# Head of an attention-plus-gated-MLP kernel: one load on another queue, one sum split around a transpose, three weight tiles for one

## The chip, the cores and the metric

The kernel runs on one core of one Trainium2 chip. A core has a matrix engine (TensorE, PE in the profile, with weight loads shown apart as PEld), a vector engine (VectorE, DVE), a scalar engine (ScalarE, ACT), GpSimdE (POOL) and a sync engine (SP). Each has its own instruction stream and runs it in order; they meet through semaphores. Transfers between memory and on-chip buffers are issued as instructions by SP, and a few by ACT; their issue shows in the profile as SPq and ACTq. The metric is the device time of one execution in microseconds (us). A nanosecond is written ns.

## The reference

One sequence of 2048 rows with 640 features is normalised row by row and goes through two branches, whose sums are added to the input:

```python
xn = _layernorm(x)                       # mean 0, variance 1 per row
qkv = xn @ wqkv                          # 640 x 1920: 32 heads of 20 for q, k and v
scores = q @ k.T * 20 ** -0.5            # a query sees the last 256 keys up to itself
o = softmax(masked scores) @ v           # per head
h = _sigmoid(xn @ w_gate) * (xn @ w_up)  # 640 x 1536 each
out = x + o @ wo + h @ w_down
```

Inputs, weights and output are bf16.

## The kernel before, in words

The 2048 rows are cut into four chunks of 512, and a chunk into four blocks of 128 rows. A chunk is normalised, transposed into `xnT` (features on partitions), projected to Q, K and V, and used for the gated MLP; attention runs in steps over head groups, and the MLP, the later projections and the output products are dealt out between these steps by a small planner (`Fill`) when the program is built. The schedule is written by hand: every engine gets its instructions in the order of the Python program, and nothing reorders them on the chip.

Only the head of the program is touched by the change, the first 13 us or so, in which chunk 0 is loaded, normalised and projected to V:

* **Loads.** SP issues, in this order: blocks 0, 1 and 3 of x (line 157, 160 KB each), the first half of the V columns of `wqkv` (line 161, 400 KB), block 2 of x, the second V half, then the Q and the K columns (line 151, 800 KB each). After these come MLP weights and the clearing of scratch rows. Since SP's instruction stream is in order, a later line is issued after the earlier ones.
* **Warm-up.** TensorE multiplies constants (line 233, ten 512-column products) until the first rows are there. ScalarE's first instruction is a load of its function table for the square root, placed ahead of a dummy activation (line 229) that reads `eps`, which POOL fills.
* **Normalising chunk 0.** Blocks 0 and 3 get mean and variance on VectorE (`ln_half`, `ln_mv`, lines 253 and 259); blocks 1 and 2 get theirs on ScalarE by two passes with accumulation (`mean_act`, line 620, and `root_act`, lines 625 and 626). `root` (line 610) is a square root on ScalarE, `norm` and `norm_act` (lines 614, 273, 630, 631) finish on VectorE.
* **Transposes.** `transpose_rows` (lines 280 and 281) turns a normalised block by five TensorE products with the identity, into a PSUM tile, and copies it to `xnT`; block 0 in pieces of three and two columns-of-128 by ScalarE, the other blocks whole by VectorE. These are called t0 to t3 below.
* **V.** `project_v` (line 329) makes one half (320 columns) of V for one block by five products; Vsh below is block s, half h (V00, V01, ..., V31). `copy_v` (line 338) brings the sums from PSUM into the V tiles, split between VectorE and ScalarE.

The order of TensorE's work in the head is: warm-up, t0, t1, V00, V10, t3, V01, V30, V11, t2, V31, V20, V21. After that come the Q and K projections of chunk 0 (`proj_block`, line 300), which read Q and K columns of the same weight tile, and then the long mixed part. The one weight tile `wqkv` has 3 x 640 columns for each of the five 128-feature slices.

Of the kernel before, what the change touches and what calls it, by code (L numbers as in the profile page):

```python
# [9 lines left out]
P = 128  # L10
S = 2048
D = 640
# [3 lines left out]
DC = D // P  # L16
FC = F // P
CW = 512
# [7 lines left out]
HALF = 320  # L26
# [11 lines left out]
BF16 = mybir.dt.bfloat16  # L38
FP32 = mybir.dt.float32
EXP = mybir.ActivationFunctionType.Exp  # L40
TANH = mybir.ActivationFunctionType.Tanh
SQRT = mybir.ActivationFunctionType.Sqrt
# [51 lines left out]
def kernel(  # L94
# [11 lines left out]
    nc = tc.nc  # L106
# [4 lines left out]
    def pool(name, bufs, **kw):  # L111
        return ctx.enter_context(tc.tile_pool(name=name, bufs=bufs, **kw))

    const = pool("const", 1)
# [13 lines left out]
    ps_d = pool("ps_d", 4, space=bass.MemoryType.PSUM)  # L128
# [10 lines left out]
        xc[c] = t  # L139
        nc.sync.dma_start(out=t, in_=xr[:, c * SBC:(c + 1) * SBC, :])  # L140

    wqkv = const.tile([P, DC, 3 * D], BF16, name="wqkv")
    wqkv_r = A_wqkv.rearrange("(c p) n -> p c n", p=P)
    wg = [const.tile([P, DC, FS], BF16, name=f"wg{k}") for k in range(F // FS)]
    wu = [const.tile([P, DC, FS], BF16, name=f"wu{k}") for k in range(F // FS)]
# [2 lines left out]

    ones = nc.const_aps.tensor(1.0, [P, CW], BF16)
    def load_wqkv(part):  # L150
        nc.sync.dma_start(out=wqkv[:, :, part * D:(part + 1) * D],
                          in_=wqkv_r[:, :, part * D:(part + 1) * D])

    xc[0] = xp.tile([P, SBC, D], BF16, name="xc")

    def load_rows(s, queue):
        queue.dma_start(out=xc[0][:, s, :], in_=xr[:, s, :])  # L157

    def load_v(hf):
        a = 2 * D + hf * HALF  # L160
        nc.sync.dma_start(out=wqkv[:, :, a:a + HALF], in_=wqkv_r[:, :, a:a + HALF])

    load_rows(0, nc.sync)
    load_rows(1, nc.sync)
    load_rows(3, nc.sync)
    load_v(0)
    load_rows(2, nc.sync)
    load_v(1)
    load_wqkv(0)
    load_wqkv(1)  # L170

    scratch = {(w, k): tc.dram_tile([H * 32, CW], BF16, name=f"s{w}{k}")
# [52 lines left out]
    nc.gpsimd.memset(neghalf, -0.5)  # L225
    eps = const.tile([P, 1], FP32, name="eps")
    nc.gpsimd.memset(eps, EPS)
    scr = const.tile([P, 1], FP32, name="scr")
    nc.scalar.activation(out=scr, in_=eps, func=SQRT)
    for n in (6, 4):  # L230
        ps = ps_d.tile([P, CW], FP32, name="pwarm", tag="d")
        for k in range(n):
# [14 lines left out]
    xnT = {}  # L247
    xns = {}

    def ln_half(c, s, a, stats=None):  # L250
        if a == 0:
            stats = lnp.tile([P, 2, nc.vector.BN_STATS_DIM], FP32, name="stats")
        nc.vector.bn_stats(out=stats[:, a, :], in_=xc[c][:, s, a * HALF:(a + 1) * HALF])
        return stats

    def ln_mv(stats, mv=None):
        if mv is None:
            mv = lnp.tile([P, nc.vector.BN_AGGR_DIM], FP32, name="mv")
        nc.vector.bn_aggr(out=mv, in_=stats)
        return mv  # L260
# [16 lines left out]
    def transpose_rows(s, copy, lo=0, hi=DC):  # L277
        pt = ps_h.tile([P, DC, P], BF16, name="pt", tag="h")
        for d in range(lo, hi):
            nc.tensor.transpose(pt[:, d, :], xns[0, s][:, d * P:(d + 1) * P], ident)  # L280
        copy(out=xnT[0][:, lo:hi, s * P:(s + 1) * P], in_=pt[:, lo:hi, :])

    def turn_block(c, s):
        nc.sync.dma_start(out=xnT[c][:, :, s * P:(s + 1) * P], in_=xns.pop((c, s)), transpose=True)
# [5 lines left out]
    qk = {}  # L290
    vt = {}

    def proj_block(w, c, m):


        base = 0 if w == "q" else D
        ps = ps_d.tile([P, CW], FP32, name="pqk", tag="d")
        for d in range(DC):
            wt = wqkv[:, d, base:base + D].rearrange("p (k m) -> p m k", m=DC)
            nc.tensor.matmul(ps, lhsT=wt[:, m, :], rhs=xnT[c][:, d, :],  # L300
                             start=(d == 0), stop=(d == DC - 1))
        st = stp.tile([P, CW], BF16, name="st")
        if w == "q":
            nc.vector.tensor_copy(out=st, in_=ps)
        else:
            nc.scalar.copy(out=st, in_=ps)
        dst = scratch[w, c % 2].rearrange("(h j) s -> h j s", j=32)
        nc.sync.dma_start(out=dst[:, 4 * m:4 * m + 4, :], in_=st)
# [14 lines left out]
        nc.gpsimd.memset(v[:, :, 0:16 * VW].rearrange("p k (h d) -> p k h d", d=VW)[:, :, :, DH:VW], 0.5)  # L323
        nc.gpsimd.memset(v[:, :, 16 * VW:], 0.0)

    def project_v(c, s, hf, home=ps_d, tag="d"):
        ps = home.tile([P, CW], FP32, name="pv", tag=tag)
        for d in range(DC):
            nc.tensor.matmul(ps[:, 0:HALF], lhsT=xnT[c][:, d, s * P:(s + 1) * P],  # L329
                             rhs=wqkv[:, d, 2 * D + hf * HALF:2 * D + (hf + 1) * HALF],  # L330
                             start=(d == 0), stop=(d == DC - 1))
        return ps

    def copy_v(c, s, hf, ps, copy, us=(0, 1)):

        v = vt[c * SBC + s][hf * U:(hf + 1) * U, :, 0:16 * VW].rearrange("p k (h d) -> p k h d", d=VW)
        for u in us:
            copy(out=v[:, u, :, 0:DH],  # L338
                 in_=ps[u * U:(u + 1) * U, 0:HALF].rearrange("p (h d) -> p h d", d=DH))

    def proj_v(c, s, hf, copy):
        copy_v(c, s, hf, project_v(c, s, hf), copy)
# [26 lines left out]
    def g_qk(c):  # L369
        for w in "qk":  # L370
            for m in range(DC):
                proj_block(w, c, m)
                if c == 0 and w == "q" and m == 1:
                    load_x(1)
                if c == 0 and w == "q" and m == 3:
                    load_gu(wu, B_w_up, 0, FS // 2)
                if c == 1 and w == "q" and m == 3:
                    load_wo()
                if c and w == "k" and m == 1:
                    spread("q", c, 0, GH)  # L380
                yield 5 * MM
        if c == 0:
            spread("q", c, 0, 2)
            spread("k", c, 0, 2)
            spread("q", c, 2, 4)
            spread("k", c, 2, 4)
# [96 lines left out]
    def scores(c, o, step):  # L483
        pt = pp.tile([P, HG, PTW], BF16, name="pT")
        ps = ps_s.tile([P, HG, CW], FP32, name="ps")
        for j, q, n, col in step["pieces"]:
            kc, kb = divmod(c * CW // U + j, CW // U)
            for a in range(2):
                for i in range(HG):
                    nc.tensor.matmul(  # L490
                        ps[a * U:(a + 1) * U, i, col * U:(col + n) * U],
                        lhsT=qk["k", kc, o // GH][32 * i:32 * i + DH, o % GH + a, kb * U:(kb + 1) * U],
                        rhs=qk["q", c, o // GH][32 * i:32 * i + DH, o % GH + a, q * U:(q + n) * U],
                        start=True, stop=True)
        width = step["units"] * U
        nc.scalar.activation(out=pt[:, :, 0:width], in_=ps[:, :, 0:width], func=EXP, scale=SCALE)  # L496
        if "late" in step:
            u = step["late"]
            view = pt[:, :, u * U:(u + 2) * U]
            return pt, lambda: nc.vector.tensor_tensor(out=view, in0=view, in1=edge, op=MIN)  # L500

        for (u, n), base, sign in ((step["diag"], 0, 1), (step["old"], -1, -1)):
            for a in range(2):
                two = pt[a * U:(a + 1) * U].rearrange("p h (a b) -> p h a b", a=2)
                k, b = divmod(u, SPAN)
                view = two[:, :, k:k + n, b * U:(b + 1) * U]
                nc.gpsimd.affine_select(out=view, in_=view, pattern=[[0, HG], [0, n], [sign, U]],  # L507
                                        compare_op=GE, fill=0.0, base=base, channel_multiplier=-sign)
        return pt, None
# [98 lines left out]
    def root(mv):  # L608
        r = lnp.tile([P, 1], FP32, name="rstd")
        nc.scalar.activation(out=r, in_=mv[:, 1:2], func=SQRT, bias=eps)  # L610
        return r
# [17 lines left out]
    def norm_act(s, xn, neg, r):  # L629
        nc.vector.reciprocal(r, r)  # L630
        nc.vector.tensor_scalar(out=xn, in0=xc[0][:, s, :], scalar1=neg[:, 0:1],  # L631
                                scalar2=r[:, 0:1], op0=ADD, op1=MULT)
        xns[0, s] = xn
# [4 lines left out]
    act, dve = nc.scalar.copy, nc.vector.tensor_copy  # L638
# [6 lines left out]
    for lo, hi in ((0, 3), (3, DC)):  # L645
        transpose_rows(0, act, lo, hi)
    norm_act(1, xn1, neg1, r1)
    mv3 = ln_mv(ln_half(0, 3, 1, stats3))
    transpose_rows(1, dve)
    v00 = project_v(0, 0, 0)  # L650
    r3 = root(mv3)
    xn2, neg2 = mean_act(2)
    r2 = root_act(2, xn2, neg2)
    norm(3, mv3, r3)
    v10 = project_v(0, 1, 0)
    copy_v(0, 0, 0, v00, dve, (0,))
    transpose_rows(3, dve)
    v01 = project_v(0, 0, 1)
    norm_act(2, xn2, neg2, r2)
    copy_v(0, 0, 0, v00, act, (1,))  # L660
    copy_v(0, 1, 0, v10, act)
    v30 = project_v(0, 3, 0, ps_h, "h")
    copy_v(0, 0, 1, v01, act)
    v11 = project_v(0, 1, 1)
    copy_v(0, 3, 0, v30, act)
    transpose_rows(2, dve)
    v31 = project_v(0, 3, 1, ps_h, "h")
    copy_v(0, 1, 1, v11, dve)
    copy_v(0, 3, 1, v31, act)
# [52 lines left out]
    for t, (c, k, o, step) in enumerate(todo):  # L722
# [11 lines left out]
        pt, late = scores(c, o, step)  # L734
# [12 lines left out]
    c = NCH - 1  # L747
# [62 lines left out]
```

## Time and profile before

| what | value |
|---|---|
| median of three runs | 309.67 us (309.5 to 310.33) |
| the profiled execution | 309.64 us, of which the span of instructions is 307.9 us |
| TensorE busy in the span | 300.4 us (98%) |
| ScalarE, VectorE, POOL busy | 198.4 us, 171.2 us, 168.7 us |
| warm-up products | first at 0.84 us |
| first transpose of chunk 0 (t0) | 5.54 us |
| first V product | 6.96 us |
| first Q product | 13.20 us |

The times inside the span count from its start. The 1.7 us between the span and the execution's time lie outside all instructions. A row of a timeline merges instructions of the same line that stand next to each other: it shows the start of the first, the length, the engine, the line, the operation, the tile written and the tiles read, the number of instructions, and in square brackets the idle time of the engine before the row and what ended it. TensorE's products are pipelined: a listed 380 ns for a 512-column product is its latency, while one starts about every 216 ns.

### The profile page before, as it was taken

What the parts mean: (1) busy time and instruction counts of PE and PEld (TensorE: products, weight loads), DVE (VectorE), ACT (ScalarE), POOL (GpSimd) and SP (SyncE); (2) the same over time, 40 slices, a digit from 0 to 9 for tenths busy, and PEclk for the clock granted to TensorE, in tenths of its full rate; (3) what the DMA queues carried; (4) which work ended last, traced back from release to release, by engine and by line L of the source; (5) the groups of instructions that cost most, each with busy time, mean ns of one, the idle gap of its engine ahead of it and who ended that gap; (6) DMA issues with size and microseconds to landing.
All of it is one profiled execution on the core that took longest, in us unless ns stands there. A gap on an engine that the chain in (4) does not pass through costs nothing.

```text
span 307.9 us, 9937 instructions
## 1 busy us (share of the span) xinstructions
PE 300.4 (98%) x4276; PEld 167.7 (54%) x4311; DVE 171.2 (56%) x339; ACT 198.4 (64%) x197; POOL 168.7 (55%) x308
## 2 busy tenths in 40 slices
PE   7999999999999999999999999999999999999995
PEld 3654444555657654554457654554546664444774
DVE  4633667648698364487946164383734536363523
ACT  6923877698854649888674547878585547688000
POOL 6000686687874828576672728457372937566000
PEclk9999999999999999999999999999999999999999
DMA  7997986984709363630015312650000200000202
GB/s 220 366 319 237 333 161 199 351 228 144 234 2 127 69 179 124 189 109 2 3 24 87 87 57 87 209 162 0 3 2 2 86 27 21 2 2 6 84 21 67
DMA packets 40460, 35.68 MB, mean 116 GB/s; under 512 B 10560, under 2 KB 39872, under 8 KB 40384
## 3 DMA queue, kind: packets, MB, share of 16 engines
q1 hardware_dynamic: 39552, 34.27, 38.6%
q10 hardware_dynamic: 864, 0.77, 0.8%
q8 instruction: 34, 0.56, 0.8%
q14 instruction: 10, 0.08, 0.1%
HBM read 23.63 MB, written 10.26 MB: 110 GB/s over the span
## 4 chain that ended last, share of the span: by engine, by line
PE 96%; issue 1%; DMA 1%; ACT 1%; DVE 0%; SPq 0%
PE y L435 18%; PE pu L421 17%; PE pg L414 17%; PE pqk L300 14%; PE ps L490 9%; PE pv L329 7%; PE y L442 7%; PE acc L523 6%; DMA xc<-in_A_x_dram 1%; PE pt L280 0%; ACT xn L620 0%; ACT xn L625 0%; DVE xn L631 0%; SPq L157 0%; ACT rstd L626 0%
## 5 line engine op out<-in xcount | busy, mean ns | idle before, releaser
L507 POOL TENSOR_SCALAR_AFFINE_SELECT pT<-pT 64x512 bf16<-64x512 bf16 (+1 forms) x256 | 157.1, 614 | 109.1 <-ACT pT L496 96.6
L496 ACT ACTIVATE pT<-ps 128x2048 bf16<-128x2048 f32 (+1 forms) x76 | 141.0, 1855 | 59.8 <-PE ps L490 57.9
L425 DVE SCALAR_TENSOR_TENSOR h<-th,pu 128x512 bf16<-128x512 f32 x48 | 32.8, 683 | 51.4 <-PE pu L421 44.9
L421 PE MATMUL pu<-xnT,wu 128*128 128x512 bf16 x228 | 59.0, 380 | 0.7 <-issue 0.2
L414 PE MATMUL pg<-xnT,wg 128*128 128x512 bf16 x226 | 58.5, 380 | 0.9 <-issue 0.3
L435 PE MATMUL y<-wd,h 128*128 128x320 bf16 (+2 forms) x396 | 56.8, 295 | 0.0
L300 PE MATMUL pqk<-xnT,wqkv 128*128 128x512 bf16 x191 | 45.4, 381 | 0.6 <-issue 0.2
L435 PEld LDWEIGHTS <-h 128*128 128x128 bf16 x396 | 36.7, 98 | 15.9 <-issue 1.8
L417 ACT ACTIVATE th<-pg 128x512 f32<-128x512 f32 x48 | 28.6, 595 | 15.5 <-PE pg L414 15.4
L414 PEld LDWEIGHTS <-wg 128*128 128x128 bf16 x240 | 22.3, 98 | 25.8 <-issue 2.0
L421 PEld LDWEIGHTS <-wu 128*128 128x128 bf16 x240 | 22.0, 98 | 25.5 <-issue 2.0
L300 PEld LDWEIGHTS <-wqkv 128*128 128x128 bf16 x200 | 22.5, 119 | 18.7 <-issue 1.4
L535 DVE STREAM_TRANSPOSE t<-acc 128x512 f32<-128x512 f32 x32 | 21.1, 696 | 20.1 <-PE acc L523 20.1
L490 PE MATMUL ps<-qT,kT 20*64 20x320 bf16 (+4 forms) x1440 | 32.1, 260 | 0.0
L490 PEld LDWEIGHTS <-kT 20*64 20x64 bf16 x1440 | 15.4, 103 | 24.9 <-issue 21.8
L446 DVE SCALAR_TENSOR_TENSOR rows<-y,rows 128x320 bf16<-128x320 f32 x30 | 14.4, 488 | 25.9 <-PE y L442 25.7
L547 DVE TENSOR_TENSOR on<-t,rec 128x320 bf16<-128x320 f32 (+4 forms) x48 | 27.8, 579 | 1.1
L329 PE MATMUL pv<-wqkv,xnT 128*128 128x320 bf16 x160 | 25.8, 300 | 0.0
L442 PE MATMUL y<-wo,oc 128*128 128x320 bf16 (+2 forms) x165 | 24.2, 295 | 0.0
L338 DVE CAST v<-pv 64x320 bf16<-64x320 f32 x29 | 14.1, 486 | 12.5 <-PE pv L329 12.3
L523 PE MATMUL acc<-pT,v 64*32 64x320 bf16 (+4 forms) x1440 | 19.7, 253 | 0.0
L523 PEld LDWEIGHTS <-v 64*32 64x32 bf16 x1440 | 16.2, 91 | 5.8 <-ACT pT L496 1.7
(48 smaller groups left out, 157.3 us busy)
## 6 DMA issues: line engine op xcount, KB each, us to landing
qT<-sq SPq DMA_DIRECT2D x16, 256.0 KB
kT<-sk SPq DMA_DIRECT2D x16, 256.0 KB
sq<-st SPq DMA_DIRECT2D x20, 128.0 KB
sk<-st SPq DMA_DIRECT2D x20, 128.0 KB
out_dram<-rows SPq DMA_DIRECT2D x15, 160.0 KB
wg<-in_B_w_gate_dram SPq DMA_DIRECT2D x4, 480.0 KB
wu<-in_B_w_up_dram SPq DMA_DIRECT2D x4, 480.0 KB
xc<-in_A_x_dram SPq DMA_DIRECT2D x3, 640.0 KB
```

The costliest lines, as they stand in the source:

```text
L300: nc.tensor.matmul(ps, lhsT=wt[:, m, :], rhs=xnT[c][:, d, :], start=(d == 0), stop=(d == DC - 1))
L329: nc.tensor.matmul(ps[:, 0:HALF], lhsT=xnT[c][:, d, s * P:(s + 1) * P], rhs=wqkv[:, d, 2 * D + hf * HALF:2 * D + (hf + 1) * HALF], start=( ...
L414: nc.tensor.matmul(pg, lhsT=part(wg, d, f), rhs=xnT[c][:, d, :], start=(d == 0), stop=(d == DC - 1))
L417: nc.scalar.activation(out=th, in_=pg, func=TANH, scale=0.5)
L421: nc.tensor.matmul(pu, lhsT=part(wu, d, f), rhs=xnT[c][:, d, :], start=(d == 0), stop=(d == DC - 1))
L425: nc.vector.scalar_tensor_tensor(out=h, in0=th, scalar=1.0, in1=pu, op0=ADD, op1=MULT)
L435: nc.tensor.matmul(y[:, 0:cut[1] - cut[0]], lhsT=ht[c, f][:, s * P:(s + 1) * P], rhs=wd[:, f, cut[0]:cut[1]], start=(f == 0), stop=False)
L442: nc.tensor.matmul(y[:, 0:cut[1] - cut[0]], lhsT=oc[c, m][:, s * P:(s + 1) * P], rhs=wo[:, m, cut[0]:cut[1]], start=False, stop=(m == DC - 1))
L490: nc.tensor.matmul(ps[a * U:(a + 1) * U, i, col * U:(col + n) * U], lhsT=qk["k", kc, o // GH][32 * i:32 * i + DH, o % GH + a, kb * U:(kb + ...
L496: nc.scalar.activation(out=pt[:, :, 0:width], in_=ps[:, :, 0:width], func=EXP, scale=SCALE)
L507: nc.gpsimd.affine_select(out=view, in_=view, pattern=[[0, HG], [0, n], [sign, U]], compare_op=GE, fill=0.0, base=base, channel_multiplier ...
L523: nc.tensor.matmul(acc[32 * i:32 * i + 32, q * U:(q + n) * U], lhsT=vt[kb][a * U:(a + 1) * U, u, h * VW:h * VW + 32], rhs=pt[a * U:(a + 1) ...
```

## The change

* The load of x block 2 is issued by ScalarE instead of SP. In ScalarE's stream it stands behind the table load and the dummy activation, which now come ahead of all loads in the program and read a constant 1.0 in place of `eps`. The load is no longer between the two V halves in SP's stream.
* `wqkv` becomes three tiles, one each for Q, K and V, filled by the same four transfers.
* V00 is split: its first three products stand ahead of t1, its last two behind. The copy of t1 is split as well: three of its five columns-of-128 by VectorE, two by ScalarE.
* V01 moves ahead of t3, and V11 ahead of V30; ScalarE's copies of V00, V10, V01 and V30 keep their order. TensorE's order becomes: warm-up, t0, three products of V00, t1, two products of V00, V10, V01, t3, V11, V30, t2, V31, V20, V21.

```diff
-    wqkv = const.tile([P, DC, 3 * D], BF16, name="wqkv")
+    wqkv = [const.tile([P, DC, D], BF16, name="w" + part) for part in "qkv"]
...
-        nc.sync.dma_start(out=wqkv[:, :, part * D:(part + 1) * D],
-                          in_=wqkv_r[:, :, part * D:(part + 1) * D])
+        nc.sync.dma_start(out=wqkv[part], in_=wqkv_r[:, :, part * D:(part + 1) * D])
...
     def load_v(hf):
-        a = 2 * D + hf * HALF
-        nc.sync.dma_start(out=wqkv[:, :, a:a + HALF], in_=wqkv_r[:, :, a:a + HALF])
-
+        a = hf * HALF
+        nc.sync.dma_start(out=wqkv[2][:, :, a:a + HALF], in_=wqkv_r[:, :, 2 * D + a:2 * D + a + HALF])
+
+    scr = const.tile([P, 1], FP32, name="scr")
+    nc.scalar.activation(out=scr, in_=nc.const_aps.tensor(1.0, [P, 1], FP32), func=SQRT)
+    load_rows(2, nc.scalar)
     load_rows(0, nc.sync)
     load_rows(1, nc.sync)
     load_rows(3, nc.sync)
     load_v(0)
-    load_rows(2, nc.sync)
     load_v(1)
...
-    scr = const.tile([P, 1], FP32, name="scr")
-    nc.scalar.activation(out=scr, in_=eps, func=SQRT)
...
-        copy(out=xnT[0][:, lo:hi, s * P:(s + 1) * P], in_=pt[:, lo:hi, :])
+        copies = copy if isinstance(copy, tuple) else ((lo, hi, copy),)
+        for a, b, cp in copies:
+            cp(out=xnT[0][:, a:b, s * P:(s + 1) * P], in_=pt[:, a:b, :])
...
-    def project_v(c, s, hf, home=ps_d, tag="d"):
-        ps = home.tile([P, CW], FP32, name="pv", tag=tag)
-        for d in range(DC):
+    def project_v(c, s, hf, home=ps_d, tag="d", lo=0, hi=DC, ps=None):
+        if ps is None:
+            ps = home.tile([P, CW], FP32, name="pv", tag=tag)
+        for d in range(lo, hi):
             nc.tensor.matmul(ps[:, 0:HALF], lhsT=xnT[c][:, d, s * P:(s + 1) * P],
-                             rhs=wqkv[:, d, 2 * D + hf * HALF:2 * D + (hf + 1) * HALF],
+                             rhs=wqkv[2][:, d, hf * HALF:(hf + 1) * HALF],
...
-    transpose_rows(1, dve)
-    v00 = project_v(0, 0, 0)
+    v00 = project_v(0, 0, 0, hi=3)
+    transpose_rows(1, ((0, 3, dve), (3, DC, act)))
+    project_v(0, 0, 0, lo=3, ps=v00)
     r3 = root(mv3)
     xn2, neg2 = mean_act(2)
     r2 = root_act(2, xn2, neg2)
     norm(3, mv3, r3)
     v10 = project_v(0, 1, 0)
     copy_v(0, 0, 0, v00, dve, (0,))
+    v01 = project_v(0, 0, 1)
     transpose_rows(3, dve)
-    v01 = project_v(0, 0, 1)
     norm_act(2, xn2, neg2, r2)
     copy_v(0, 0, 0, v00, act, (1,))
     copy_v(0, 1, 0, v10, act)
+    v11 = project_v(0, 1, 1)
+    copy_v(0, 0, 1, v01, act)
     v30 = project_v(0, 3, 0, ps_h, "h")
-    copy_v(0, 0, 1, v01, act)
-    v11 = project_v(0, 1, 1)
+    transpose_rows(2, dve)
     copy_v(0, 3, 0, v30, act)
-    transpose_rows(2, dve)
     v31 = project_v(0, 3, 1, ps_h, "h")
```

More of the change, by code (lines that the diff above doesn't have):

```diff
@@ L293, in proj_block @@
     def proj_block(w, c, m):
-        base = 0 if w == "q" else D
         ps = ps_d.tile([P, CW], FP32, name="pqk", tag="d")
         for d in range(DC):
-            wt = wqkv[:, d, base:base + D].rearrange("p (k m) -> p m k", m=DC)
+            wt = wqkv["qk".index(w)][:, d, :].rearrange("p (k m) -> p m k", m=DC)
             nc.tensor.matmul(ps, lhsT=wt[:, m, :], rhs=xnT[c][:, d, :],
```

## The prediction

> **What bounds the kernel now.** The first view is the page's busy shares and its chain of work that ended last.
>
> ```profile
> PE 300.4 (98%) x4276; PEld 167.7 (54%) x4311; DVE 171.2 (56%) x339; ACT 198.4 (64%) x197; POOL 168.7 (55%) x308
> ...
> PE 96%; issue 1%; DMA 1%; ACT 1%; DVE 0%; SPq 0%
> ```
>
> TensorE is the bound: 96% of the chain is its own work. It follows a fixed order with hardly a gap, so a microsecond won or lost by TensorE in the head should move the end by as much, and nothing else there counts. The second view is the chain in order of time, for the head.
>
> ```profile
> 1.25 2.52 DMA xc<-in_A_x_dram
> ...
> 3.79 0.83 ACT xn L620 x2
> 4.62 0.18 ACT rstd L610
> 4.80 0.82 ACT xn L625 x2
> ...
> 6.17 0.46 DVE xn L631
> ...
> 6.67 0.45 PE pt L280 x5
> 7.13 1.44 PE pv L329 x10
> 8.56 0.28 PE pt L280 x5
> 8.84 2.12 PE pv L329 x15
> ```
>
> Each line has its start, its length and what ran. Up to 6.67 us the end hangs on block 1 of x: its load, ScalarE's two passes, VectorE's normalising. From then on it is TensorE alone. Third, the timeline of the head by engine:
>
> ```profile
> 3.18 0.89 DVE L253 BATCH_NORM_STATS2 stats<-xc 128x6 f32<-128x320 bf16 x2 [3.18 <-DMA xc<-in_A_x_dram]
> ...
> 3.79 0.74 ACT L620 ACTIVATE xn<-xc 128x640 bf16<-128x640 bf16 x1 [0.79 <-DMA xc<-in_A_x_dram]
> ...
> 6.67 0.45 PE L280 MATMUL pt<-ident,xn 128*128 128x128 bf16 x5 [0.57 <-DVE xn L631]
> ...
> 7.71 0.52 PEld L329 LDWEIGHTS <-xnT 128*128 128x128 bf16 x5 [0.24 <-DVE xnT L281]
> ...
> 283.56 0.39 ACTq L452 DMA_DIRECT2D rows<-in_A_x_dram  x1
> ```
>
> Block 0 lands at 3.18, block 1 at 3.79. The gap that can be won is TensorE's 0.57 us ahead of 6.67. Behind it V10 waits 0.24 for t1's copy as PEld counts it; the chain's ten products in 1.44 and fifteen in 2.12 (and fifteen more in 2.12 from 11.24), against 136 ns each (1.36 and 2.04), show 0.08 us of stall three times, 0.24 in all. Everything that could be gained up to the first Q product is 0.57 + 0.24 = 0.81 us, or 0.26% of the time.
>
> The profiled execution took 309.64 us (span 307.9 and 1.7 around it), 0.03 under the median of 309.67; I add shifts to 309.64. A difference of 0.3%, 0.93 us, is about what this kernel's runs can tell from no change.
>
> **Part 1: three products of V00 ahead of t1.** They need ScalarE's copy of t0's first three columns: start 6.03, 479 ns by its form's row, so 6.51. The products start at about 6.57 (the 0.06 us that V10 takes behind its copy now), each 136 ns: until 6.98. Block 1's normalised rows are ready at 6.62, so t1 now stands behind V00 and moves from 6.67 to 6.98. Its five transposes take 0.28 as at 8.56, and two products of V00 follow: TensorE is through with them at 7.53 instead of 7.63. That is the whole gain, 0.10, if V10 could start then.
>
> **Part 2: the split copy of t1.** V10 waits for it. Now the copy starts 0.48 us after its transposes start (t3: 8.40 to 8.88; t2: 10.80 to 11.28). Behind 6.98 VectorE's part starts between 7.36 (it waits for the third transpose alone, 0.11 less) and 7.46 (for all five). No row has a 384-column copy by VectorE: the 640-column one takes 475 to 492 ns, so it lies between 0.285 (in proportion) and 0.49; I take 0.35, since it does most of the same work with a fixed part in it. It ends between 7.65 and 7.95, mine 7.76; ScalarE's 256 columns take 377 ns as in t0's second piece, until about 7.84, in time for V10's fourth product. V10 starts at 7.82, between 7.71 and 8.01, where it now starts at 7.76. So V00's gain is eaten by its own delay of t1: -0.05 to +0.25, mine +0.06.
>
> ScalarE's copy stands ahead of the root of block 3, which starts at 7.30 now, and would start at 7.76: everything queued behind it on ScalarE (the root, block 2's two passes) is 0.46 later. Block 3's rows come at 8.71 instead of 8.27. V01 ahead of t3 covers that: V10 ends at 8.50, V01 at 9.18, and t3 starts then; uncovered it would cost 0.2. Block 2's rows come at 10.73 instead of 10.27, and t2 starts at about 10.88 (V11 9.46 to 10.14, then a stall of 0.06 for t3's copy, then V30): 0.15 us of cover left, and beyond it a loss one for one. Behind t2 the order is the old one. Against 10.80 now, TensorE is 0.08 later, bounds -0.1 to +0.3. V00's, V10's and V01's copies on ScalarE move 0.5 later; they run without a gap until 14.4, and the next work of ScalarE is at 19.87, so this is hidden, and the PSUM tiles they free are needed by Q blocks behind 14.
>
> **Part 3: block 2's load on ScalarE's queue.** SP issues block 2 at 2.66 for 0.53 us now; what stands behind on SP (second V half at 3.22, Q and K at 3.70, MLP weights at 5.65) is issued that much earlier. It gains nothing: the 16 engines are about full from 5 us on, and Q's first product is at 13.20. Summing the moved bytes in quarter microseconds, 0.328 MB (blocks 0 and 1) were through at 3.10 and landed at 3.79, so a load lands about 0.65 after its bytes. By order of issue, the first V half (0.90 MB in all) is through at 5.37 and lands at 6.0; if block 2's 0.164 MB come ahead of it, 6.5. It was needed at 6.91, now at 6.55: cover of 0.05 to 0.5. Late, it would hold t1 as well, at most 0.3; I take 0, since the engines moved only 151 and 97 GB/s between 3.75 and 4.25, where block 2 fits in. The second V half (1.475 MB) lands at 7.7, needed at 8.50.
>
> What counts is when ScalarE issues it. If the table load (0.79, 1.28 us) holds the queue, it is issued at 2.1, its bytes flow from about 3.1 (block 0 was issued at 0.80, its bytes flowed from 1.8), and block 1 is already through: no cost. If not, it is issued at 0.9 beside block 0, and pushes block 1, on the chain above: by 0.6 at most (0.492 MB were through at 3.71 against 0.328 at 3.10), by 0 if a second queue raises the rate to the 390 GB/s of 8 to 9 us; 0.4 in between, since the rate was near 280 there. The one row that bears on it is ACT's issue at 283.56, in the middle of an activation that ran from 282.32 to 284.20: the queue doesn't wait for a running activation. For a table load nothing is shown. The two cases are close to even; I take the first, as a table load is no activation, and keep both.
>
> The Trainium skill (Perfetto Trace Analysis, Sequencer Loop) says that a sequencer pushes engine instructions into a queue and goes on, and only rarely does special work for one itself. By that rule the second case is the rule and the sum would be +0.5; the row at 283.56 agrees for an activation, and no run here shows the table load. The skill (DMA: Bandwidth & Descriptors, Queues, rings and completion order) adds that the engines take turns between queues packet by packet, which would make block 2 halve block 0's and 1's rate; no row of the head shows two queues.
>
> The dummy activation no longer waits for eps (0.72 us of idle, off the chain): nothing.
>
> **Part 4: weight tiles.** Same transfers, same products, same strided reads of Q and K columns (117 ns per weight load, under 216 per product): nothing, as long as the loads move at the old rate; Q has 3 us and more of cover. No V product waits for Q or K now, so no wait is removed.
>
> **Sum.** +0.08, or 309.72: 309.7, own range 309.5 to 310.0.
>
> **Rivals.**
> *The load runs ahead of the table load* (the change doesn't do what it says): 309.72 + 0.4 = 310.1, up to 310.3. For: the row at 283.56. Against: the table load may be handled otherwise.
> *V00 fills the gap for good*: if VectorE's copy takes 0.285 and three stalls of 0.08 go, 309.64 - 0.05 - 0.24 = 309.35. The bound of 0.81 allows no more than 308.8. Against: t3's and t2's copies still have one product group ahead of them.
> *TensorE's fast clock comes later* (slower): the warm-up products start every 0.43 us, the Q products every 0.216, and t0's first transpose still takes 311 ns against 219: TensorE speeds up at about 5.7 us, in t0. Its gap between the warm-up's last product (0.84 + 10 x 0.427 = 5.11) and t0 is 0.43 now. If block 0 lands 0.4 later, it is 0.8; if that makes the speed-up miss its moment, TensorE runs at half speed for up to another 4.9 us, a loss of 2.4; half of that, 1.2, decides for slower: 311.3 to 312.1. Against: a gap of 0.57 follows t0 now without harm.
> The Trainium skill (TensorE: Matmul & The Clock Gate, part 1) has a free-running window of 3.4 us that must be busy before the clock doubles; an estimate by it is a loss of 1.7 us for one window. The 4.9 us here agree with a start inside one window.
>
> **How the numbers follow.** The forecast 0.50, the load running ahead 0.34, the gap filled 0.08, the clock 0.08. Slower by over 0.3% are the clock's 0.08 and 0.03 of the load's with a late V half; faster by over 0.3% is beyond the bound of 0.81 but for something unseen: 0.03. Same: 0.86. The range goes from the gap's 309.2 to 310.6, the load's 310.3 and 0.3 for a late V half.
>
> **What would show it.** Right: ScalarE's issue of block 2 at 2.1 or later, block 1's first pass at 3.8; V00's first product near 6.57, t1 near 6.98, V10 near 7.8, t2 near 10.9, Q's first product within 0.2 of 13.20, and the same distance to the end. Wrong: an issue near 0.9 with block 1 at 4.0 or later; t0 with all five transposes slow; t1 held by V00's wait for weights; or Q's product earlier than 13.0.

## The result, and the profile after

The changed kernel takes 313.09 us (median of seven executions, 310.84 to 314.0) against 310.21 us (309.5 to 310.46) for the kernel before: a ratio of 1.0081, 95% interval 1.0058 to 1.0105. A second measurement, beside other kernels, gave 1.0078 (1.0055 to 1.0102). By these ratios the change makes the kernel slower by some 2.5 us (the medians differ by 2.9), where 309.7 us and no change had been forecast.

The profiled execution took 313.09 us, its span is 311.3 us. First the page's busy shares and the chain of work that ended last:

```profile
PE 302.9 (97%) x4276; PEld 168.9 (54%) x4311; DVE 171.3 (55%) x339; ACT 198.8 (64%) x198; POOL 169.1 (54%) x308
...
PE 94%; DVE 2%; DMA 2%; issue 1%; SPq 0%; DVEq 0%
PE y L435 17%; PE pu L421 16%; PE pg L414 16%; PE pqk L299 14%; PE ps L490 8%; PE pv L329 8%; PE y L442 7%; PE acc L523 6%; DMA wv<-in_A_wqkv_dram 2%; DVE h L425 1%; DVE on L547 1%; DVE xn L272 0%; PE pt L279 0%; SPq L156 0%; DVE oc L551 0%
```

A load of V weights (`wv`) stands in the chain with 2%, where blocks of x stood before. The chain in order of time (start, length, what) shows the head:

```profile
2.18 5.71 DMA wv<-in_A_wqkv_dram
7.89 0.04 issue
7.93 0.96 PE pv L329 x3
8.89 0.53 PE pt L279 x5
9.42 3.30 PE pv L329 x12
...
13.19 1.44 PE pv L329 x10
...
14.90 2.12 PE pv L329 x15
17.02 0.21 PE pqk L299
```

Two things stand in it. V00's first product waits for the first half of the V weights until 7.9; in the kernel before TensorE was at work on t1 at 6.67 and on V00 at 6.96. And the fifteen products that follow take 0.96 + 3.30 = 4.26 us, 0.28 each, where the last fifteen take 2.12, 0.14 each: TensorE runs at half speed until about 13. The clock record that the trace keeps says when: it begins with the first change to full speed, which is at 12.99 us here and at 5.82 us in the kernel before. Q starts at 17.02 in the chain, against 13.36 before: 3.66 us lost in the head, and the span is 3.4 us longer. The last exponential (line 496) starts at 286.00 us, against 282.32 before, so the whole loss is carried through the kernel; 0.3 us of it comes back in what follows. Of the 3.66, 1.26 lie ahead of 7.93 (against t1 at 6.67), and 2.40 behind it, where the half speed is.

Third, the timeline of the head by engine:

```profile
0.80 1.28 ACT L163 ACT_TABLE_LOAD   x1 [0.80 <-PEq L795]
0.86 0.39 ACTq L156 DMA_DIRECT2D xc<-in_A_x_dram  x1
...
3.36 0.89 DVE L252 BATCH_NORM_STATS2 stats<-xc 128x6 f32<-128x320 bf16 x2 [3.36 <-DMA xc<-in_A_x_dram]
...
4.11 0.74 ACT L620 ACTIVATE xn<-xc 128x640 bf16<-128x640 bf16 x1 [1.82 <-DMA xc<-in_A_x_dram]
...
5.97 0.71 PE L279 MATMUL pt<-ident,xn 128*128 128x128 bf16 x5 [0.71 <-DVE xn L272]
7.93 0.96 PE L329 MATMUL pv<-wv,xnT 128*128 128x320 bf16 x3 [1.24 <-DMA wv<-in_A_wqkv_dram]
...
9.85 0.37 ACT L282 COPY xnT<-pt 128x256 bf16<-128x256 bf16 x1 [2.58 <-DVE xnT L282]
```

ScalarE issues block 2's load at 0.86, 0.06 us into its table load, not behind it. Block 0 lands at 3.36 instead of 3.18, block 1 at 4.11 instead of 3.79. The last line is a wait that had not been foreseen: ScalarE's part of t1's copy waits for VectorE's part.

### The profile page after: what moved, and what is told of

The parts are those of the page before. It is cut to its first block, busy times and chain, and to the rows that moved or that the text cites. A ratio compares the mean times of both kernels' runs of the same rounds, so it can differ in the third digit from the quotient of the medians.

```text
span 311.3 us, 9939 instructions
## 1 busy us (share of the span) xinstructions
PE 302.9 (97%) x4276; PEld 168.9 (54%) x4311; DVE 171.3 (55%) x339; ACT 198.8 (64%) x198; POOL 169.1 (54%) x308
## 4 chain that ended last, share of the span: by engine, by line
PE 94%; DVE 2%; DMA 2%; issue 1%; SPq 0%; DVEq 0%
PE y L435 17%; PE pu L421 16%; PE pg L414 16%; PE pqk L299 14%; PE ps L490 8%; PE pv L329 8%; PE y L442 7%; PE acc L523 6%; DMA wv<-in_A_wqkv_dram 2%; DVE h L425 1%; DVE on L547 1%; DVE xn L272 0%; PE pt L279 0%; SPq L156 0%; DVE oc L551 0%
## 5 line engine op out<-in xcount | busy, mean ns | idle before, releaser
L329 PE MATMUL pv<-wv,xnT 128*128 128x320 bf16 x160 | 28.0, 316 | 1.2 <-DMA wv<-in_A_wqkv_dram 1.2
L299 PE MATMUL pqk<-xnT,wk 128*128 128x512 bf16 x97 | 23.1, 381 | 0.2
L299 PE MATMUL pqk<-xnT,wq 128*128 128x512 bf16 x94 | 22.8, 381 | 0.4 <-issue 0.2
L329 PEld LDWEIGHTS <-xnT 128*128 128x128 bf16 x160 | 15.2, 102 | 10.9 <-issue 1.6
```

## The experiments

Three theories stood at the start. Theory 1: the early issue of block 2 makes blocks 0 and 1 and the V half late, and the gaps in TensorE's work then cost it its full speed. Theory 2: the three weight tiles make the V half late. Theory 3: V00 ahead of t1 costs, whatever the queue. Ratios are to the kernel before on the same chip, with their 95% intervals.

### Block 2 back on SP, all else as changed

```diff
-    load_rows(2, nc.scalar)
...
     load_v(0)
+    load_rows(2, nc.sync)
     load_v(1)
```

> The changed kernel, with block 2's load back on SP between the two V halves; order of TensorE, split copy and three tiles stay. Theory 1 (the queue: block 2's bytes run beside blocks 0 and 1, the first transposes and the V half come late, and TensorE misses its speed-up): t0 back at 5.5, V00 at 6.6 to 6.9, TensorE at full speed by 6; 309.9 to 310.6. Theory 2 (the three tiles make the V half land later): V00 still waits to about 7.9 for its weights; 312 or more. Theory 3 (V00 ahead of t1 holds t1 whatever the queue): t1 at 7.3 or later, a loss of 0.5 to 1: 310.7 to 311.2.

Measured: ratio 1.0018 (0.9995 to 1.0042), median 310.4 us; t0 at 5.51, V00 at 6.93 behind a wait of 0.71 for its weights, t1 at 7.34, first Q product at 13.92. The queue is most of the loss: this interval ends at 1.0042, that of the changed kernel begins at 1.0058. Not all of theory 1's expectation holds: the V half lands at 6.9 even without block 2's early bytes, so V00 doesn't reach the gap it was meant for, and t1 is held by it to 7.34, as theory 3 has it.

### The queue alone

```diff
+    scr = const.tile([P, 1], FP32, name="scr")
+    nc.scalar.activation(out=scr, in_=nc.const_aps.tensor(1.0, [P, 1], FP32), func=SQRT)
+    load_rows(2, nc.scalar)
     load_rows(0, nc.sync)
...
     load_v(0)
-    load_rows(2, nc.sync)
...
-    scr = const.tile([P, 1], FP32, name="scr")
-    nc.scalar.activation(out=scr, in_=eps, func=SQRT)
```

> The kernel before, with nothing changed but block 2's load, which ScalarE issues behind its table load and a dummy activation on a constant. Theory 1: issue at 0.86, block 0 at 3.36, block 1 at 4.1, t0 at 5.97 at half speed, V00's weights at 7.9, half speed until about 12.9: nearly the whole loss, 312 to 313.5. Theory 2: the old tile lands in time, blocks 0 and 1 are 0.2 to 0.3 late: 310.5. Theory 3: t1 isn't held behind V00, so 310.5 to 311.

Measured: ratio 1.0042 (1.0018 to 1.0066), median 311.92 us. It shows a loss without tiles or order, between theory 1's expectation and those of the others. Whether it is smaller than the full one the ratios leave open, as the intervals overlap. The profile is of its slowest execution (313.28 us). The issue is at 0.86, block 1's first pass at 4.21, V00 at 7.77 behind a wait for its weights, first Q product at 15.51 instead of 13.20. Here the granted clock in the table of windows (stretch; its length, busy time of PE, PEld, DVE, ACT and POOL; then the clock, the DMA share and GB/s) shows TensorE's half speed:

```profile
7.50:8.00 0.50, 0.27 (x3) 0.18 (x2) 0.50 (x2) 0.28 (x2) 0.00 (x0) 1.00 1.00 325
8.00:8.50 0.50, 0.50 (x4) 0.27 (x3) 0.46 (x3) 0.50 (x2) 0.00 (x0) 0.56 0.97 339
...
11.00:11.50 0.50, 0.50 (x4) 0.27 (x3) 0.48 (x2) 0.34 (x1) 0.00 (x0) 0.52 1.08 385
11.50:12.00 0.50, 0.50 (x5) 0.38 (x4) 0.45 (x1) 0.04 (x1) 0.00 (x0) 1.00 1.07 362
```

The transposes of t0 and t1 ran at full speed here (five in 0.45 us); from about 8.06 to 11.48 (the shares of 0.56 and 0.52 worked out), 3.4 us, the clock is at half, though TensorE is at work again from 7.77 on. The clock record has the changes at 4.65 (to full), 8.06 (to half) and 11.48 (to full), 3.41 us from one to the next. In the changed kernel's own profile this column says 1.00 all through, while its products take twice their time from 7.93 to 13: there TensorE never came to full speed before. The column doesn't show the first slow stretch of an execution, since the clock record begins only where it ends: the first warm-up products start every 0.43 us under a clock of 1.00, too.

### Three tiles alone

```diff
-    wqkv = const.tile([P, DC, 3 * D], BF16, name="wqkv")
+    wqkv = [const.tile([P, DC, D], BF16, name="w" + part) for part in "qkv"]
...
```

> The kernel before, with nothing changed but three weight tiles for one. Theory 1 and theory 3: no change, 310.2 within 0.3. Theory 2: V00's weights late, V00 at 7.5 or later, 311 or more.

Measured: ratio 1.0004 (0.9983 to 1.0025); V00 at 6.81, first Q product at 13.04. Theory 2 falls; the tiles cost nothing that shows.

### The order alone

```diff
...
-    transpose_rows(1, dve)
-    v00 = project_v(0, 0, 0)
+    v00 = project_v(0, 0, 0, hi=3)
+    transpose_rows(1, ((0, 3, dve), (3, DC, act)))
+    project_v(0, 0, 0, lo=3, ps=v00)
...
+    v01 = project_v(0, 0, 1)
     transpose_rows(3, dve)
-    v01 = project_v(0, 0, 1)
...
```

> The kernel before, with nothing changed but the order: V00's three products ahead of t1, the split copy, V01 ahead of t3, V11 ahead of V30. Theory 1: t0 at 5.5, TensorE at full speed by 6; V00 at 6.6 if its weights have landed, at most at 6.9; t1's copy still in two steps one behind the other, as in the changed kernel (VectorE, then ScalarE), which costs 0.3: 310.2 to 310.8. Theory 2: no more than 0.3 from before. Theory 3: t1 held to 7.3 or later, 310.7 to 311.2.

Measured: ratio 1.0029 (1.0009 to 1.0048), median 310.97 us; V00 at 6.72, t1 at 7.13, V10 at 8.02, t2 at 11.29 (10.80 before), first Q product at 13.70. The order alone costs (the helpers for a split sum and a split copy, and V11 and t2 in their new places, are part of the edit and not printed here). In the head it is the smaller part, 0.50 us at the first Q product against 2.31 in the profile of the queue alone; the two ratios overlap and don't tell. The timeline by engine has two reasons:

```profile
6.72 0.57 PE L332 MATMUL pv<-wqkv,xnT 128*128 128x320 bf16 x3 [0.68 <-ACT xnT L283]
7.13 0.44 PE L280 MATMUL pt<-ident,xn 128*128 128x128 bf16 x5
...
8.00 0.37 ACT L283 COPY xnT<-pt 128x256 bf16<-128x256 bf16 x1 [1.28 <-DVE xnT L283]
8.27 0.30 ACT L613 ACTIVATE rstd<-mv,eps 128x1 f32<-128x1 f32 x1
```

V00's weight load from `xnT` ran at 6.50 and its product at 6.72, so the product waited for the V columns, not for the copy that the row names. And ScalarE's copy starts when VectorE's ends, with block 3's root behind it at 8.27 instead of 7.30.

The 0.50 us is less than the 0.9 of the ratio, and there is more further on. In the profiled execution (311.58 us) the last exponential is 2.15 us late: TensorE stands idle ahead of output products for 0.49 us at 85.63 and for 0.75 at 157.28, where the profile of the kernel before has no such gaps. Gaps like these stand in profiles with other heads too (0.75 us at 155.69 with three tiles alone, 0.23 at 87.44 with the queue alone). They are a second source of spread, far behind the head; what brings them was not tried.

### Block 2 on ScalarE, but held until block 0 has landed

```diff
-    scr = const.tile([P, 1], FP32, name="scr")
-    nc.scalar.activation(out=scr, in_=nc.const_aps.tensor(1.0, [P, 1], FP32), func=SQRT)
-    load_rows(2, nc.scalar)
...
     nc.gpsimd.memset(eps, EPS)
+    scr = const.tile([P, 1], FP32, name="scr")
+    nc.scalar.activation(out=scr, in_=eps, func=SQRT)
+    load_rows(2, nc.scalar)
```

> The changed kernel, with block 2's load still issued by ScalarE, but behind the old dummy activation on eps and behind the landing of block 0: ScalarE's stream then stands still until about 3.2, which its table load did not make it do. Theory 1 (an issue at 0.86 puts block 2's bytes beside blocks 0 and 1): issue near 3.2, block 0 at 3.2, block 1 at 3.6 to 3.8, t0 at 5.5; block 2's bytes now run beside the V half, whose landing is 6.9 (as with the load on SP) to 7.8 (as with the issue at 0.86); 310.3 to 311.5. Rival (a second queue as such slows the loads): V00 at 7.8 or later and the time at 312 or more.

Measured: ratio 1.0008 (0.9990 to 1.0027), median 309.93 us. What holds the load is not in the edit's lines: the built program makes it wait on the semaphore that block 0's load raises, and block 0 lands at 3.15. The second queue, the tiles and the order are all still there; only the issue is at 3.15 instead of 0.86, and the loss is gone within the interval. The bytes move later still: ScalarE's queue has block 2's packets from 6.31 to 7.62 us, with the V half in by 6.43; in the changed kernel it has them from 2.18 to 3.23. Theory 1 had expected them beside the V half, and 310.3 us or more. The timeline of ScalarE's queue and TensorE:

```profile
3.15 0.43 ACTq L156 DMA_DIRECT2D xc<-in_A_x_dram  x1
3.63 0.74 ACT L620 ACTIVATE xn<-xc 128x640 bf16<-128x640 bf16 x1 [0.62 <-DMA xc<-in_A_x_dram]
...
5.51 0.45 PE L279 MATMUL pt<-ident,xn 128*128 128x128 bf16 x5 [0.46 <-DVE xn L272]
6.43 0.58 PE L329 MATMUL pv<-wv,xnT 128*128 128x320 bf16 x3 [0.46 <-ACT xnT L282]
6.84 0.44 PE L279 MATMUL pt<-ident,xn 128*128 128x128 bf16 x5
```

V00's first product is at 6.43, right behind the copy, and t1 at 6.84: here the change does what the prediction's first part works out. Even so the first Q product is at 13.42, 0.22 later than before, and this is the profile of its fastest execution (309.56 us).

### TensorE kept busy in the changed kernel

```diff
-    for n in (6, 4):
+    for n in (6, 6):
...
+    ps = ps_d.tile([P, CW], FP32, name="pwarm", tag="d")
+    for k in range(5):
+        nc.tensor.matmul(ps, lhsT=ones[:, 0:P], rhs=ones, start=(k == 0), stop=(k == 4))
     v00 = project_v(0, 0, 0, hi=3)
```

> The changed kernel with more products of constants on TensorE, whose results nothing reads: twelve in place of ten ahead of t0, and five more between t0 and V00. They change no load. Theory 1 (a part of the loss is TensorE at half speed after its gaps at 5.1 to 6.0 and 6.7 to 7.9): the V half still lands near 7.9, but from there TensorE runs at full speed; first Q product at 15.0 in place of 17.0; 311.5 to 312.2 and all runs within 1 us of each other. Rival (the products are slow because their operands are, or because the loads take the memory): V products stay at 0.27 us each until about 12.9, and 313 or more.

Measured: ratio 1.0058 (1.0039 to 1.0077), eight executions from 310.94 to 312.22 us. V00 follows the added products at 7.55 without a wait of its own, and the V products run at full speed; the first Q product is at 14.53, not 16.86. None of the eight executions has a mean granted clock under 0.998; of the 22 with the early load and without the added products (the changed kernel, measured twice, and the queue alone) 13 have 0.995 or less. In the profiles, then, more work on TensorE makes this kernel's head faster; for the whole time, 1.0058 against 1.0081 and 1.0078, the intervals overlap.

```profile
6.17 0.45 PE L279 MATMUL pt<-ident,xn 128*128 128x128 bf16 x5 [0.17 <-DVE xn L272]
6.46 1.25 PE L651 MATMUL pwarm<-const-bfloat16-1.0 128*128 128x512 bf16 x5
7.55 0.57 PE L329 MATMUL pv<-wv,xnT 128*128 128x320 bf16 x3
...
8.85 1.53 PE L329 MATMUL pv<-wv,xnT 128*128 128x320 bf16 x10 [0.18 <-DVE xnT L282]
```

So the slow products are TensorE's speed, not their operands or the loads: the rival falls. The rest, about 1.3 us at the first Q product (14.53 against 13.20), is the late data, the order and what the added products themselves hold up; the run doesn't part them.

### Eleven products of constants in the kernel before

```diff
-    for n in (6, 4):
+    for n in (6, 5):
```

> The kernel before with eleven products of constants in place of ten, whose results nothing reads: TensorE's gap ahead of t0 goes from 0.43 to nothing. Theory 1 (the kernel before, too, loses in some executions to a late speed-up): runs above 311 vanish, the lowest stays at 309.5, median 309.7 to 310.0. Rival (ten are enough, and the spread has other reasons): median 310.2 within 0.15, and runs above 311 as before.

Measured: ratio 0.9993 (0.9972 to 1.0013). None of ten executions is above 311 us (the highest is 310.55), against 5 of 29 of the kernel before beside it. That points to theory 1, but ten executions are too few to show it, and the median is the same (309.81 against 309.75). Nor is a late speed-up the only candidate. The profile here is of the highest execution, 310.55 us: its first Q product is at 13.08, earlier than before, and its last exponential 0.74 late, with TensorE idle for 0.37 us at 84.87 ahead of output products. The five executions above 311 all have a mean clock of 1.000, which such a gap and a late first speed-up both leave as it is.

### The order alone, t1 in two PSUM tiles

```diff
-    transpose_rows(1, ((0, 3, dve), (3, DC, act)))
+    transpose_rows(1, dve, 0, 3)
+    transpose_rows(1, act, 3, DC)
```

> The kernel before with the new order alone, but t1 goes into two PSUM tiles, one for VectorE's copy and one for ScalarE's, so that the second copy needn't wait for the first. Theory 1 (the order costs by that wait): ScalarE's copy at 7.4 to 7.6 in place of 8.0, V10 at 7.7, block 3's root at 7.9 in place of 8.3, first Q product at 13.3; ratio to before 1.000 to 1.001 in place of 1.003. Rival (the order costs because t1 stands behind three products of V00): V10 at 8.0 or later, ratio 1.003 as before.

Measured: ratio 1.0015 (0.9995 to 1.0035); the lines above are against the order-alone kernel. ScalarE's copy at 7.66 follows TensorE and no longer VectorE, V10 starts at 7.97 instead of 8.02, block 3's root is at 7.93 instead of 8.27, the first Q product at 13.45 instead of 13.70, though V00 starts at 6.78, 0.06 later than there.

```profile
7.66 0.37 ACT L283 COPY xnT<-pt 128x256 bf16<-128x256 bf16 x1 [0.93 <-PE pt L280]
7.93 0.30 ACT L613 ACTIVATE rstd<-mv,eps 128x1 f32<-128x1 f32 x1
```

In the profiles the serial copy costs 0.25 us; the two ratios overlap and don't tell it. Of what is left at the first Q product, 0.25, V00's wait for its weights makes 0.11 (it starts at 6.78, where t1 started at 6.67 before). Most of the rest is V10's wait for VectorE's copy, which ends at 7.91: V10's first product starts 0.37 us after the one ahead of it, where products otherwise start 0.14 apart. V10 thus comes much as the rival has it, and the ratio (1.0015) lies between the two expectations.

### The three flaws mended together

This is the held load, t1 in two tiles, and eleven products of constants, in the changed kernel.

> The changed kernel with its three flaws mended: block 2's load held on ScalarE until block 0 has landed, t1 in two PSUM tiles so that the two copies don't wait for each other, eleven products of constants ahead of t0. Theory 1 (early bytes, the serial copy and the late speed-up are the whole loss): the new order is then worth what V00's start in the gap is worth, 0.0 to 0.2: first Q product at 13.0 to 13.2, ratio to before 0.997 to 1.000, no run above 311. Rival (standing ahead of t1 costs by itself): ratio 1.001 or more, first Q product at 13.4 or later.

Measured: ratio 0.9997 (0.9986 to 1.0008), eleven executions from 309.31 to 310.08 us. The loss is gone, and nothing is gained. The ratio is as theory 1 has it, the first Q product is not: it comes at 13.74, 0.54 later than before and where the rival had it. In its profile (309.89 us) the V half lands at 7.07, and V00 waits 1.11 for it:

```profile
5.51 0.45 PE L279 MATMUL pt<-ident,xn 128*128 128x128 bf16 x5 [0.84 <-DVE xn L272]
...
7.07 0.57 PE L329 MATMUL pv<-wv,xnT 128*128 128x320 bf16 x3 [1.11 <-DMA wv<-in_A_wqkv_dram]
...
13.74 3.62 PE L299 MATMUL pqk<-xnT,wq 128*128 128x512 bf16 x16
```

With the same loads the V half had landed by 6.43 in the held kernel. Its landing differs by 0.6 us between executions, and V00's place ahead of t1 gains or loses with it.

The gaps ahead of t0 and of V00, 0.84 and 1.11, are no smaller in sum than those of the queue alone (0.94, 0.68 and 0.23), yet the clock stays full behind them, and all eleven executions have a mean clock of 0.998 or more. So gaps of this size make a fall possible, not certain.

### Nine products of constants in the kernel before

```diff
-    for n in (6, 4):
+    for n in (6, 3):
```

> The kernel before with nine products of constants in place of ten: the gap ahead of t0 goes from 0.43 to 0.86, as in the changed kernel, and no load moves. Theory 1 (such a gap makes TensorE's speed-up uncertain): more runs above 311 than the one in six of the kernel before, median 310.3 to 311.5. Rival (only the late V half matters): median and spread as before.

Measured: ratio 1.0013 (0.9994 to 1.0032), median 310.0 against 309.63; two of ten executions are above 311, six of 29 of the kernel before. A gap ahead of t0 alone doesn't bring a loss of the changed kernel's size; the profile has t0 at full speed (five transposes in 0.45) behind a gap of 0.71. Inconclusive for so small an effect.

### The changed kernel once more

> The changed kernel once more, beside the three others on one chip. Theory 1: ratio to before 1.007 to 1.010 and a spread of 3 us, against 1.3 us where TensorE is kept busy. Rival (the first measurement had more late speed-ups than is usual): ratio 1.006 or less, as where TensorE is kept busy.

Measured: ratio 1.0078 (1.0055 to 1.0102), six executions from 311.48 to 313.45 us. The profile has the early issue (0.85), block 1's first pass at 4.46, V00 at 7.26, and a half-speed stretch at another place than the first profile, from about 8.66 (0.83 of full clock in that microsecond) to 12.08:

```profile
8.00:9.00 1.00, 0.82 (x7) 0.31 (x4) 0.36 (x1) 0.47 (x2) 0.00 (x0) 0.83 1.06 380
...
12.00:13.00 1.00, 1.00 (x9) 0.71 (x8) 0.92 (x3) 0.96 (x3) 0.00 (x0) 0.96 1.09 334
```

The mean granted clock of four of its six executions is 0.993 or 0.994 over a span of 310 us, which is a stretch of about 4 us at half speed (0.0065 x 310 / 0.5), near the 3.4 us of the windows. The other two have 0.999 and 1.000 and are the slowest. That fits the first profile, whose clock is 1.000 too: where full speed comes only long after V00, the column doesn't show the slow stretch. In the first measurement both kinds occur too: the slowest execution, 314.0, has 0.989, the fastest, 310.84, has 1.000.

### The held load alone

```diff
     scr = const.tile([P, 1], FP32, name="scr")
     nc.scalar.activation(out=scr, in_=eps, func=SQRT)
+    load_rows(2, nc.scalar)
...
     load_v(0)
-    load_rows(2, nc.sync)
```

> The kernel before with the load of block 2 alone moved to ScalarE, held there until block 0 has landed. Theory 1 (the early issue is what costs, not the second queue): within 0.1% of before, where the same move with an early issue gave 1.004; t1 and V00 as before, first Q product at 13.0 to 13.2. Rival (a second queue costs as such): 1.002 or more, V00 later than 7.1.

Measured: ratio 0.9996 (0.9978 to 1.0015); V00 at 6.85, t2 at 10.80, first Q product at 13.21.

```profile
3.13 0.45 ACTq L157 DMA_DIRECT2D xc<-in_A_x_dram  x1
...
6.85 1.60 PE L329 MATMUL pv<-wqkv,xnT 128*128 128x320 bf16 x10
```

Beside the ratio of 1.0042 for the same move with the early issue this settles the main point: the queue as such costs nothing that shows, the time of the issue does. It gains nothing either. Block 2 now comes later (its first pass waits 0.48 for the load, until 7.96), and t2 is where it was.

## Why the prediction was wrong, point by point

**What bounds the kernel** held: 3.66 us lost by TensorE ahead of the first Q product came out as 3.4 us of span. That nothing else counts did not hold in every execution: the profile of the order alone loses 0.50 us in the head and 2.15 by the last exponential.

**Part 1, three products of V00 ahead of t1.** The mechanism is as worked out where the weights are there (6.43 and 6.84 in the held kernel, for 6.57 and 6.98). The premise that they are there was wrong; see part 3.

**Part 2, the split copy.** VectorE's 384 columns took 0.36 us, for 0.35. The step that failed is "ScalarE's 256 columns ... until about 7.84": it took the two copies to run side by side. Both read one PSUM tile, and the program makes the second wait for the first. In the order-alone kernel t2 is 0.49 later than before, against the forecast of 0.08 with bounds up to 0.3; with two PSUM tiles it is 0.25. A reading was wrong without harm: ScalarE's next instruction behind the V copies is a table load at 14.42, not the work at 19.87, but 3.95 us of idle time follow it.

**Part 3, block 2's load.** Three steps failed here.

First, "I take the first, as a table load is no activation". The load went out at 0.86, 0.06 us into the table load. The row at 283.56 had shown ScalarE's queue issuing during an activation; it was the only row that bore on the question, and the forecast set it aside. The Trainium skill (Perfetto Trace Analysis, Sequencer Loop), which has a sequencer push engine instructions into a queue and go on, was right for a table load too; the 0.86 agrees. The sum had this case as a rival with 0.34.

Second, the term for the V half: "by order of issue ... lands at 6.0; if block 2's 0.164 MB come ahead of it, 6.5", and "late ... at most 0.3; I take 0". Where V00 was seen to wait, the half came at 6.72, 6.78, 6.93 and 7.07 without the early load and at 7.3 to 7.9 with it; in the held kernel it was there by 6.43. The working laid the transfers end to end. By the sums of the windows about 1.34 MB had moved when the half landed at 6.89 with block 2 on SP, and 1.62 MB at 7.89 in the changed kernel, against 0.90 and 1.065 MB up to its end in order of issue: later transfers move beside earlier ones, so a sum of bytes gives no more than an early bound. Why the early load delays the half by up to 1 us, more than its 0.164 MB take, was not tried and stays open. It is not that the V columns move late as a whole: the 640th of their 640-byte packets, and a half has 640, has ended by 5.90 in the changed kernel and by 5.92 with block 2 on SP. The records don't tell the packets of the two halves apart.

Third, the size of the run-ahead rival: blocks 0 and 1 were later by 0.2 to 0.5 and 0.3 to 0.7, much as its 0.4 has it, but its 310.1 left out what follows: the V half and the clock.

**Part 4, weight tiles,** held: 1.0004.

**The rivals.** *TensorE's fast clock comes later* had the right mechanism, and its price for the clock fits (a loss up to 2.4; 2.40 us lie behind 7.93 in the profile), with a chance of 0.08. Its time, 311.3 to 312.1, stays below the measured 313.09, as it left out the late V half. The failing step is that it was counted as a case of its own beside the run-ahead, though its condition, a later block 0, is just what the run-ahead brings: with the early issue 13 of 22 executions have a mean clock of 0.995 or less, and the first profile shows a slow stretch that this figure misses. Its condition was also too narrow. The gap ahead of t0 alone does little (nine products: 1.0013, not clear of zero). The gaps ahead of t0 and of V00 together can cost the clock, as filling both shows; they need not, as the three flaws mended show, with gaps of 0.84 and 1.11 us and no fall. What decides stays open. The Trainium skill (TensorE: Matmul & The Clock Gate, part 1) has a free-running window of 3.4 us for the clock; the steps of 3.41 us in the clock record of the queue-alone kernel agree with it, and so does the start of the half speed at different times in different executions (8.06 there, 8.66 in the changed kernel once more).

*V00 fills the gap for good* did not come true even with all three flaws mended: 0.9997.

## What to carry to other kernels

A load on ScalarE's queue went out here at 0.86 us, with the table load and the activation ahead of it not yet done; if such a load must come late, give it something to wait for. In a head where several loads are due within a microsecond, a load issued earlier on another queue can make all of them late (here blocks 0 and 1 and the V half), so ask which of them the first matrix products wait for. And when TensorE's start slips, price the slip with its clock: in the profiles the first Q product is 1.3 us late with TensorE kept busy (14.53 against 13.20), and 2.3 more without (16.86 against 14.53).

## What the runs showed of the hardware that was not expected

* A transfer behind a table load on ScalarE's queue is issued 0.06 us after the table load has begun (0.80 and 0.86, in three kernels and four profiles), and the dummy activation starts 0.01 us after the 1.28 us of the table load.
* TensorE can fall back to half speed for 3.4 us after gaps of less than a microsecond each: 0.94, 0.68 and 0.23 us idle ahead of t0, t1 and V00 in the queue-alone kernel, with work between them. The fall comes later than the gaps, at 8.06, when TensorE is busy again. It comes 3.41 us after the change to full speed at 4.65; in the changed kernel once more the record has 5.25, 8.67 and 12.08. Gaps of 0.84 and 1.11 us in the kernel with all three flaws mended brought no fall.
* The moment of full speed differs between profiles whose warm-up starts alike, at 0.83 or 0.84 us: by the clock record 3.48 us in the kernel with all three flaws mended, 4.65 in the queue alone, 5.82 (in t0) in the kernel before, and 12.99 and 5.25 in two profiles of the changed one.
* The mean granted clock of a run tells of such a stretch (0.994 or 0.995 against 1.000), but not of one in which full speed had not yet been reached.
